# A state-space block and a maxout network on one core: another order of the opening, sixteen unread products, other tables for blocks zero and one

## The chip, the cores and the metric

The kernel runs on one core of a Trainium2 chip. The metric is the device time of one execution in microseconds; lower is better. A run gives one time; the numbers here are medians of a few runs, and one further execution is recorded by the hardware profiler.

Engines go by these names: PE is TensorE (matmul; PEld is its weight load), DVE is VectorE, ACT is ScalarE, POOL is GpSimd, SP is SyncE, which here issues nearly all transfers.

## What is computed

First a chunked state-space scan over x, with decays a and projections B and C (4 batches, 8 heads, 768 tokens, head width 32, state width 16). Its output, seen as 3072 tokens of 256 numbers, goes through a network whose hidden layer is the maximum of three products.

```python
for c in range(nc):
    la = log_a[:, :, sl]
    cum = np.cumsum(la, axis=-1)
    L = np.exp(cum[:, :, :, None] - cum[:, :, None, :]) * causal
    CB = np.einsum('bhin,bhjn->bhij', Cc, Bc)
    y_intra = np.einsum('bhij,bhjd->bhid', CB * L, xc)
    y_inter = np.einsum('bhin,bhnd->bhid', Cc, state) * np.exp(cum)[:, :, :, None]
    y[:, :, sl] = y_intra + y_inter
    Bx = np.einsum('bhjn,bhjd->bhjnd', Bc, xc) * decay_from_j[:, :, :, None, None]
    state = decay_full[:, :, None, None] * state + np.sum(Bx, axis=2)

h = np.maximum(np.maximum(x @ w1, x @ w2), x @ w3)
return (h @ w_out).astype(np.float32)
```

The weights w1, w2, w3 (256 by 768) and w_out (768 by 256) come as 64-bit floats and are decoded on the chip to 32 bits.

## The kernel before

The 768 tokens of a sequence are cut into six blocks of 128 (NC = 6), numbered zero to five. A block is one scan chunk of 128 tokens in all four batches and, for the network, 512 tokens.

**The order is written by hand.** The tile scheduler is off (`manual_schedule`); each engine does its instructions in the order in which the program emits them, and waits on semaphores where one needs another's result. That order is given by strings of short words. `begin` reads the words of the opening, `act` those of the lists FIRST (block zero's network: one entry behind each of 18 groups of products), SEAM and PRELUDE (between blocks zero and one), SECOND (block one: one entry behind each of 18 units), STEADY (blocks two to four) and LAST (block five).

**Opening.** The decays of block zero are needed as exp(cum_i - cum_j) in a tile L for each batch and head. For batches 0 and 1 TensorE makes the whole difference in PSUM: a mask (`spread_mask`, L398), the sums of token i (`spread_i`, L414) and those of token j (`spread_j`, L426); ScalarE takes the exponential (`first_exps`, L446). For batches 2 and 3 TensorE spreads only the i part (L414 again), GpSimd prepares the other with the mask (`below`, L433), VectorE adds them (`first_sums`, L441), and ScalarE takes the exponential. Meanwhile C and B of block zero come in halves of two batches (C0 is C of batches 0 and 1, and so on), are transposed on TensorE (L511) and copied out by ScalarE, C twice with a parity factor (L883), B once (L879). Scores (L584) are products of both; VectorE multiplies them into L (`scan_weight`, L592). For two of the four heads' pairs of batches 2 and 3 ScalarE copies the scores to SBUF (L890) and GpSimd multiplies (L892). Then come the outputs y of block zero (L627, copied at L634) and the state product A (L552).

The word `P` is a product that nobody reads: `pad` (L910) multiplies the identity with the mask into the PSUM bank of group 0, which group 0 overwrites later.

**Weights.** Twelve pieces of 512 KB are fetched by `fetch` (word W, L195). `decode` (word d) does two ScalarE passes (L220, L229), two VectorE passes (L221, L224) and an addition on GpSimd (L230); `sign` (word g) ends it on VectorE (L233). Group n of FIRST (four products, L683; groups 0 and 1 in halves, L675) needs piece n // 2. Its result is copied by ScalarE (L1166) or taken into a maximum by VectorE (L1170). From block one on each weight is used in three parts, made by the word w with the steps 0 (ScalarE, L267 and L269), 1 (L273 on VectorE or L277 on GpSimd) and 2 (L262); `WEIGHTS_DVE` lists the parts that go to VectorE.

**Running sums.** For the later blocks the decays' sums are scanned on VectorE (word r, L353), stored to DRAM (L895) and read back spread over the partitions as L tables (`decay_load`, L466, 1 MB each) and as E (`last_load`, L474, eight small transfers). GpSimd masks the tables (L478), ScalarE takes the exponentials in sets of four (word p, L485).

**Units.** In blocks one to five a unit is two products of the difference part (`unit_open`, L724), scaled in place by ScalarE (L710), and then four products of the other parts (L746). Units are opened ahead, in a ring of four PSUM banks. `LATE` names the units behind whose own products the next opening stands, instead of ahead of them; `COPIES` names those whose first result ScalarE copies (L756) rather than VectorE (L758). Down products (L783 for block zero, L788 later) lead to the output.

SP issues its transfers in program order, too; the prelude loop that fetches C, B, x and the first weight pieces stands ahead of everything else.

Of the kernel before, what the change touches and what calls it, by code (L numbers as in the profile page):

```python
# [20 lines left out]
def kernel(  # L21
# [22 lines left out]
    NB, NH, S, D = x.shape  # L44
    N = B.shape[-1]
    P = 128
    NC = S // P
# [26 lines left out]
    BACK = ((1.0 + TAU) / TAU) ** 2  # L74
    SMALL, LARGE = 2.0 ** -15, 122880.0 - 2.0 ** -7

    COPIES = {c: (0, 6, 7, 12,) if c == 1 else (1, 13,) for c in range(1, NC)}
    LATE = {c: (1, 2, 3, 5, 9, 13, 16, 17,) if c == 1 else (1, 3, 4, 6, 7, 9, 11, 14, 16, 17,) for c in range(1, NC)}
    WEIGHTS_DVE = ((0, 1), (0, 2), (1, 1), (1, 2), (3, 1), (4, 1), (4, 2), (6, 1), (7, 2), (8, 1), (9, 1), (9, 2), (10, 1), (10, 2), (11, 1),)

    const = ctx.enter_context(tc.tile_pool(name="const", bufs=1))
    raw = ctx.enter_context(tc.tile_pool(name="raw", bufs=1))
# [105 lines left out]
    def fetch():  # L188

        src, dt = weight_jobs.pop(0)  # L190
        rb = wraw.tile([P, 2, WCOL, 2], U32, tag="rb", name="rb")
        if dt == FP32:
            nc.sync.dma_start(out=rb[:, :, :, 0].bitcast(FP32), in_=src)
        else:
            nc.sync.dma_start(out=rb.rearrange("p k f w -> p k (f w)"), in_=src)  # L195
        fetched.append((rb, dt))
# [55 lines left out]
    def weight_parts(k):  # L252
# [6 lines left out]
        def last():  # L259
            d = wsum.tile([P, 2, WCOL], F32R, tag="w", name="wd")  # L260
            parts[k].append(d)
            (nc.vector if (k, 2) in WEIGHTS_DVE else nc.gpsimd).tensor_tensor(  # L262
                out=d.rearrange("p k f -> p (k f)"), in0=hi.bitcast(FP32), in1=lo.bitcast(FP32),
                op=ALU.subtract)

        def high():
            nc.scalar.activation(hi, w, AF.Copy, scale=HIGH * TAU)  # L267
            if (k, 1) not in WEIGHTS_DVE:
                nc.scalar.activation(lo, w, AF.Copy, scale=HIGH)  # L269

        def rest():
            if (k, 1) in WEIGHTS_DVE:
                nc.vector.scalar_tensor_tensor(  # L273
                    out=lo, in0=hi.bitcast(FP32), scalar=-1.0 / TAU, in1=w, op0=ALU.mult,
                    op1=ALU.add)
            else:
                nc.gpsimd.tensor_tensor(out=lo, in0=w, in1=lo.bitcast(FP32), op=ALU.subtract)  # L277
# [15 lines left out]
    def load_half(name, h):  # L293

        src = sources[name][0]
        if h == 0:
            load_tile(0, name)
        rows = slice(2 * h, 2 * h + 2)
        nc.sync.dma_start(  # L299
            out=blocks[0][name][:, 2 * h * NH:(2 * h + 2) * NH],  # L300
            in_=src[rows, :, 0:P, :].rearrange("b h s n -> s (b h) n"))

    for word in "C0 W B0 W C1 B1 x0 x1 W W".split():
        if word == "W":
            fetch()
        else:
            load_half(word[0], int(word[1]))
# [79 lines left out]
    def decays(c):  # L387
        Ls[c] = att.tile([P, NB, NH, P], FP32, tag="L", name="L")
        return Ls[c]
# [60 lines left out]
    L0, spread = decays(0), {}  # L450
# [278 lines left out]
    def unit():  # L729
# [3 lines left out]
        q, i = divmod(k, 3)  # L733
        late = 2 * k + g in LATE[c]

# [17 lines left out]
        if i == 0:  # L753
            m[g] = ffn.tile([P, BLK], FP32, tag="m", bufs=4, name="m")
            if 2 * k + g in COPIES[c]:
                nc.scalar.copy(out=m[g], in_=o)  # L756
# [230 lines left out]
        elif op in "GH":  # L987
            group_half(args[0], int(op == "H"))

    for word in ("k P v3 v2 C0 i2 q P i0 c0 d B0 u2 W j g b0 l e00 C1 P e10 e11 e01 s0 r x2 B1 x3 "  # L990
            "J i3 b1 c1 e21 s2 e20 x1 u3 e30 P x0 D W P P e31 y3 n y2 P X1 W o0 s3 z0 z1 W d "
            "A G0 o2 X0 W S L0 G1 H0 H1 N").split():
        begin(word)
    ncums = banks["ncums"]

# [69 lines left out]
    def plan(words, c, n):  # L1065
        for word in words.split():
            act(word, c, n)
# [4 lines left out]


    FIRST = [
        "g d d g f",
        "M11 W",
        "d M9 g",
        "F W M8 g d",
        "W",
        "d",  # L1080
        "M1 g m0,0 w0,0 t M0 b",
        "d C w1,0 M3",
        "w0,1 p0",
        "",
        "M4 d g p0",
        "g w1,1 d g p0 s0 x p0 w2,0",
        "w2,1 x w3,0 x g x",
        "",
        "E c m0,2",
        "w0,2 M2 d p0",  # L1090
        "s2 p0 B x x",
        "w1,2 M5 p0 p0 d g x w2,2 x g",
    ]
    SEAM = "y a a z z D w3,1 A x"
    PRELUDE = "b w3,2 B"
    SECOND = [
        "m0,0 E t w4,0 m0,2 C w5,0 w4,1 c w5,1 p0",
        "D",
        "",
        "w4,2 p0",  # L1100
        "w6,0",
        "w5,2 h p0 w7,0 s0 x w6,1 x r",
        "p0 w8,0 p0 D L w6,2 w9,0 w9,1",
        "",
        "h x w8,1 w7,1 p0 x D",
        "w10,0",
        "m1,0 p1 w7,2 r w8,2 s2 x p0",
        "h w9,2 m1,2 p0 x x",
        "w11,0 A p1",
        "w10,1 w10,2 x y x a z p1 a w11,1",  # L1110
        "w11,2 p1 z",
        "p1 h",
        "r",
        "l r",
    ]
    STEADY = [
        "t h E C b B c r",
# [38 lines left out]
    for n in range(NF * 3):  # L1156
        j, g = divmod(n, 2)
        q, i = divmod(j, 3)
        f = 2 * q + g
# [16 lines left out]
    downs += [(0, "0", b) for b in range(NB)]  # L1176
    plan(SEAM, 0, 1)
    plan(PRELUDE, 1, 2)
# [39 lines left out]
```

## Time and profile before

| | |
|---|---|
| runs | 275.38, 276.33, 277.6 us |
| median | 276.33 us |
| profiled execution, its own time | 276.44 us |
| its span, first to last instruction | 274.7 us |
| instructions in the span | 5403 |

The span is what the profile's times are counted in: they run from the first instruction. The rest of the profiled time lies around it. In the page a row of a group gives line, engine, operation, output and inputs, shapes and count, then busy time and mean length, then the engine's idle time ahead of those instructions and what ended it. The timeline merges like instructions in a row into one line, with the start and the length of the whole. A matmul in 32 bits is two records.

The costliest groups are the units' products: L746 with 96.6 us in 360 records, and L724 with 52.0 us in 180. The exponentials of the later blocks (L485) take 50.1 us of ScalarE in 160.

### The profile page before, as it was taken

The page shows a single profiled execution, that of the slowest core. Times are in us where ns is not written, and L with a number is a line of the kernel's source. Part 1 is how long each engine was busy: PE and PEld are TensorE (multiplying, and loading weights), DVE is VectorE, ACT ScalarE, POOL GpSimd, SP SyncE. Part 2 cuts the span into 40 slices and gives each one's busy share as a digit, 9 for nine tenths or more (in the row PEclk, how much of TensorE's full clock was granted, in tenths as well). Part 3 has the DMA queues.
Part 4 walks back from the last instruction along what each step waited for, and adds up shares of the span by engine and source line. Part 5 has one row for each costly group of instructions (what it writes and reads, how often), then busy time and mean ns, then how long its engine had stood idle before and what let it go on. Part 6 is the DMA issues. An engine that isn't in the chain of part 4 may idle for free.

```text
span 274.7 us, 5403 instructions
## 1 busy us (share of the span) xinstructions
PE 267.3 (97%) x2061; PEld 206.8 (75%) x2061; DVE 185.5 (68%) x299; ACT 180.8 (66%) x413; POOL 69.2 (25%) x69
## 2 busy tenths in 40 slices
PE   6999999998999999999999999999999999999995
PEld 3567454456878778879888879888889788899895
DVE  2554879999457799963488862588861787632882
ACT  4374949981989999736689736689744564534711
POOL 5215465655878502243000243000000000000000
PEclk9999999999999999999999999999999999999999
DMA  6899997959849685696250795200000100002002
GB/s 131 149 284 227 207 294 184 174 76 215 172 132 239 110 97 76 95 249 84 93 63 1 137 220 65 79 2 0 0 1 18 62 2 0 2 0 76 0 2 76
DMA packets 105097, 28.13 MB, mean 102 GB/s; under 512 B 75376, under 2 KB 102000, under 8 KB 105072
## 3 DMA queue, kind: packets, MB, share of 16 engines
q1 hardware_dynamic: 104768, 27.66, 50.3%
q8 instruction: 16, 0.26, 0.4%
q10 hardware_dynamic: 304, 0.13, 0.2%
q14 instruction: 9, 0.07, 0.1%
HBM read 24.54 MB, written 3.24 MB: 101 GB/s over the span
## 4 chain that ended last, share of the span: by engine, by line
PE 81%; SPq 8%; DVE 5%; DMA 2%; issue 2%; ACT 1%; ACTq 0%; DVEq 0%
PE up L746 31%; PE up L724 15%; PE o L788 13%; PE up L683 6%; SPq L195 5%; PE o L783 4%; PE s L584 4%; PE y L616 3%; SPq L299 2%; DMA raw_B<-in_B_dram 2%; PE o L815 2%; PE y L607 2%; DVE L L592 1%; PE A L552 1%; PE trB L511 1%
## 5 line engine op out<-in xcount | busy, mean ns | idle before, releaser
L746 PE MATMUL up<-six,wp 128*128 128x512 f32 x360 | 96.6, 396 | 0.0
L746 PEld LDWEIGHTS up<-six,wp 128*128 128x128 f32 x360 | 65.9, 188 | 15.0 <-issue 1.0
L760 DVE TENSOR_TENSOR m<-m,up 128x512 f32<-128x512 f32 x60 | 40.3, 684 | 42.6 <-PE up L746 42.2
L710 ACT ACTIVATE up<-up 128x512 f32<-128x512 f32 x90 | 50.6, 580 | 26.6 <-PE up L724 26.5
L724 PE MATMUL up<-six,wd 128*128 128x512 f32 x180 | 52.0, 396 | 0.0
L485 ACT ACTIVATE L<-L,ncums 128x128 f32<-128x128 f32 x160 | 50.1, 393 | 1.1 <-POOL L L478 1.1
L724 PEld LDWEIGHTS up<-six,wd 128*128 128x128 f32 x180 | 33.2, 188 | 8.7 <-issue 1.2
L592 DVE TENSOR_TENSOR L<-s,L 128x512 f32<-128x512 f32 x46 | 30.5, 685 | 9.3 <-PE s L584 8.0
L683 PE MATMUL up<-six,w 128*128 128x512 f32 x64 | 28.6, 598 | 0.7 <-DVE w L233 0.7
L478 POOL TENSOR_SCALAR_AFFINE_SELECT L<-L 128x1024 f32<-128x1024 f32 x20 | 22.9, 1166 | 10.0 <-DMA L<-cums 10.0
L788 PE MATMUL o<-wp,h 128*128 128x256 f32 x192 | 23.7, 283 | 0.0
L788 PEld LDWEIGHTS o<-wp,h 128*128 128x128 f32 x192 | 23.4, 192 | 0.1
L683 PEld LDWEIGHTS up<-six,w 128*128 128x128 f32 x64 | 11.8, 190 | 14.7 <-issue 11.8
L657 DVE SCALAR_TENSOR_TENSOR h<-h,h 128x512 fp32r<-128x512 f32 x30 | 21.7, 724 | 1.0
L230 POOL TENSOR_TENSOR h<-h,h 128x512 uint32<-128x512 uint32 x12 | 17.0, 1418 | 20.2 <-DVE h L224 19.3
L666 DVE TENSOR_TENSOR h<-m,h 128x512 fp32r<-128x512 f32 x30 | 21.2, 708 | 0.1
L663 ACT ACTIVATE h<-m 128x512 fp32r<-128x512 f32 x30 | 18.4, 629 | 3.6 <-DVE m L760 3.6
L801 ACT ACTIVATE ob<-o 128x512 f32<-128x512 f32 x10 | 6.0, 595 | 19.4 <-PE o L788 16.2
L758 DVE COPY m<-up 128x512 f32<-128x512 f32 x18 | 12.4, 687 | 7.3 <-PE up L746 7.3
L584 PE MATMUL s<-six,six 32*128 32x256 f32 x192 | 16.2, 401 | 0.0
L584 PEld LDWEIGHTS s<-six,six 32*128 32x128 f32 x192 | 10.3, 184 | 6.0 <-issue 2.4
L788 PEld LDWEIGHTS o<-wd,h 128*128 128x128 f32 x96 | 12.5, 190 | 0.7
(109 smaller groups left out, 313.7 us busy)
## 6 DMA issues: line engine op xcount, KB each, us to landing
L<-cums SPq DMA_DIRECT2D x10, 1024.0 KB, 9.4
rb<-in_moe_w_dram SPq DMA_DIRECT2D x9, 512.0 KB, 6.7
raw_x<-in_x_dram SPq DMA_DIRECT2D x5, 512.0 KB, 11.1
out_dram<-ob SPq DMA_DIRECT2D x10, 256.0 KB, 2.1
rb<-in_moe_w_out_dram SPq DMA_DIRECT2D x3, 512.0 KB, 8.1
raw_C<-in_C_dram SPq DMA_DIRECT2D x5, 256.0 KB, 6.1
raw_B<-in_B_dram SPq DMA_DIRECT2D x5, 256.0 KB, 4.2
E<-cums SPq DMA_DIRECT2D x40, 32.0 KB, 2.3
```

The costliest lines, as they stand in the source:

```text
L478: nc.gpsimd.affine_select(out=Ls[c][:, b], in_=Ls[c][:, b], pattern=[[0, NH], [1, P]], compare_op=ALU.is_ge, fill=MASKED, base=0, channel_ ...
L485: nc.scalar.activation(L[:, b, h], L[:, b, h], AF.Exp, bias=ncum[c][:, b * NH + h:b * NH + h + 1], scale=1.0)
L584: nc.tensor.matmul(out=s[:, i].rearrange("j g i -> j (g i)"), lhsT=st["BT"][rows, b], rhs=st["CT"][rows, :, b], start=(i == 0), stop=True, ...
L592: nc.vector.tensor_tensor(out=M, in0=s, in1=M, op=ALU.mult)
L657: nc.vector.scalar_tensor_tensor(out=out, in0=lo.bitcast(FP32), scalar=-1.0 / TAU, in1=hi.bitcast(FP32), op0=ALU.mult, op1=ALU.add)
L666: nc.vector.tensor_tensor(out=lo, in0=src, in1=hi.bitcast(FP32), op=ALU.subtract)
L683: nc.tensor.matmul(out=bank, lhsT=whole[3 * (f // 2) + i][:, k, f % 2 * P:(f % 2 + 1) * P], rhs=yT[0][:, k], start=(k == 0), stop=(k == KD ...
L710: nc.scalar.activation(bank, bank, AF.Copy, scale=-KAPPA)
L724: nc.tensor.matmul(out=o, lhsT=weight_part(k, 2, kk, cols), rhs=yT[c][2][:, kk], start=(kk == 0), stop=(kk == KD - 1), skip_group_check=True)
L746: nc.tensor.matmul(out=o, lhsT=weight_part(k, j, kk, cols), rhs=yT[c][j][:, kk], start=False, stop=(kk == KD - 1 and j == 1), skip_group_c ...
L760: nc.vector.tensor_tensor(out=m[g], in0=m[g], in1=o, op=ALU.max)
L788: nc.tensor.matmul(out=o[:, b % 2], lhsT=hs[f][p][:, tokens(b)], rhs=weight_part(NW + f // 2, p, f % 2, slice(0, DM)), start=(first and p ...
```

## The change

Seven places are edited; no function is.

1. The prelude loop of transfers: the first weight piece goes ahead of C0, the second behind x, and the other two of the four leave the loop for the opening.
2. The opening's words: the sums on TensorE (i0, j, i2) come directly behind the masks, ahead of the transposes of B and C; sixteen pads stand where seven were; the scan of the running sums (k, l, r) comes later; the loads of B and C of block one (X0, X1) and of the first L table (L0) move to FIRST; the second decode moves behind groups 0 and 1; weight pieces are fetched at other places.
3. FIRST: the decodes, signs, loads, weight parts, masks and scores stand behind other groups.
4. SEAM: the state product A ahead of the down product, and one order changed among the parts of y.
5. SECOND: the same words in another distribution.
6. `COPIES` and `LATE` for block one.
7. `WEIGHTS_DVE`: the parts (1,2), (4,2), (8,1), (9,1), (9,2) go to other engines, (5,2), (6,2), (7,1), (11,2) to VectorE.

```diff
-    COPIES = {c: (0, 6, 7, 12,) if c == 1 else (1, 13,) for c in range(1, NC)}
-    LATE = {c: (1, 2, 3, 5, 9, 13, 16, 17,) if c == 1 else (1, 3, 4, 6, 7, 9, 11, 14, 16, 17,) for c in range(1, NC)}
-    WEIGHTS_DVE = ((0, 1), (0, 2), (1, 1), (1, 2), (3, 1), (4, 1), (4, 2), (6, 1), (7, 2), (8, 1), (9, 1), (9, 2), (10, 1), (10, 2), (11, 1),)
+    COPIES = {c: (1, 7, 12,) if c == 1 else (1, 13,) for c in range(1, NC)}
+    LATE = {c: (3, 7, 9, 11, 12, 13, 14, 15, 16,) if c == 1 else (1, 3, 4, 6, 7, 9, 11, 14, 16, 17,) for c in range(1, NC)}
+    WEIGHTS_DVE = ((0, 1), (0, 2), (1, 1), (3, 1), (4, 1), (5, 2), (6, 1), (6, 2), (7, 1), (7, 2), (10, 1), (10, 2), (11, 1), (11, 2),)
...
-    for word in "C0 W B0 W C1 B1 x0 x1 W W".split():
+    for word in "W C0 B0 C1 B1 x0 x1 W".split():
...
-    for word in ("k P v3 v2 C0 i2 q P i0 c0 d B0 u2 W j g b0 l e00 C1 P e10 e11 e01 s0 r x2 B1 x3 "
-            "J i3 b1 c1 e21 s2 e20 x1 u3 e30 P x0 D W P P e31 y3 n y2 P X1 W o0 s3 z0 z1 W d "
-            "A G0 o2 X0 W S L0 G1 H0 H1 N").split():
+    for word in ("q i0 j v3 J i2 v2 P d e10 e11 B0 k u2 e00 g C0 c0 P b0 P e01 P l s0 B1 x0 P x1 P "
+            "C1 P c1 x3 P i3 P P P r e20 b1 D u3 s2 e21 P e31 P y2 s3 y3 e30 W x2 P z1 o0 P "
+            "z0 n A P o2 G0 G1 N H0 H1 S W d W W W").split():
...
     FIRST = [
-        "g d d g f",
-        "M11 W",
-        "d M9 g",
-        "F W M8 g d",
-        "W",
+        "g M6 M7 M10 W",
         "d",
-        "M1 g m0,0 w0,0 t M0 b",
-        "d C w1,0 M3",
-        "w0,1 p0",
-        "",
-        "M4 d g p0",
-        "g w1,1 d g p0 s0 x p0 w2,0",
-        "w2,1 x w3,0 x g x",
-        "",
-        "E c m0,2",
-        "w0,2 M2 d p0",
-        "s2 p0 B x x",
-        "w1,2 M5 p0 p0 d g x w2,2 x g",
+        "f W d g",
+        "d g",
+        "d F W M11 w0,0",
+        "d",
+        "M9",
+        "m0,0 g t g b w1,0 d g p0 m0,2",
+        "",
+        "w1,1 d C M8 W p0 w2,0 B E",
+        "w0,1 s0 W p0 x",
+        "g c w2,1",
+        "x w3,0 p0 p0 x g x w0,2 p0 w1,2 d",
+        "",
+        "",
+        "s2 d",
+        "M4 x x M0 w2,2",
+        "M3 p0 p0 M1 x g d M5 g x g M2",
     ]
-    SEAM = "y a a z z D w3,1 A x"
+    SEAM = "y a z A D a z w3,1 x"
     PRELUDE = "b w3,2 B"
     SECOND = [
-        "m0,0 E t w4,0 m0,2 C w5,0 w4,1 c w5,1 p0",
-        "D",
-        "",
-        "w4,2 p0",
-        "w6,0",
-        "w5,2 h p0 w7,0 s0 x w6,1 x r",
-        "p0 w8,0 p0 D L w6,2 w9,0 w9,1",
-        "",
-        "h x w8,1 w7,1 p0 x D",
-        "w10,0",
-        "m1,0 p1 w7,2 r w8,2 s2 x p0",
-        "h w9,2 m1,2 p0 x x",
-        "w11,0 A p1",
-        "w10,1 w10,2 x y x a z p1 a w11,1",
-        "w11,2 p1 z",
-        "p1 h",
-        "r",
-        "l r",
+        "w4,0 w4,1 w5,0 w6,0 E t c D w5,1 m0,0 C p0",
+        "",
+        "w6,1 L w4,2 w5,2 w7,0 s0 p0",
+        "w8,0",
+        "",
+        "p0 h",
+        "m1,0 w9,0 p0 m0,2",
+        "w9,1 x",
+        "x r x D p0 w6,2 w10,0 l p0 p0 w8,1 p1 x D w7,1 w7,2",
+        "",
+        "s2 m1,2 x w8,2 p1 x p0 x h w9,2",
+        "w11,0 x w10,1 p1",
+        "r w11,1 A x",
+        "w10,2 y a a z z p1",
+        "h",
+        "",
+        "w11,2 h r",
+        "r p1",
     ]
```

The words that the argument uses: P pad; q the factors from token j to the block's end (ScalarE, L361) and J their turn on TensorE; i0, i2, i3 the sums of batches 0 and 1, of 2, of 3; j the sums of token j; v below; u first sums; e an exponential (e10: batch 1, half 0); C, B, c, b transposes and copies; s scores; x, z score products on VectorE; y the same through GpSimd; o outputs; A state product; G, H halves of groups 0 and 1; M, L, X, E loads.

## The prediction

> **What bounds the kernel now.** I read the page first, then the chain of waits, then TensorE's timeline from the first product on, and last the timelines of ScalarE, VectorE and the SP queue for the same stretch. The page:
>
> ```profile
> span 274.7 us, 5403 instructions
> PE 267.3 (97%) x2061; PEld 206.8 (75%) x2061; DVE 185.5 (68%) x299; ACT 180.8 (66%) x413; POOL 69.2 (25%) x69
> PE 81%; SPq 8%; DVE 5%; DMA 2%; issue 2%; ACT 1%; ACTq 0%; DVEq 0%
> ```
>
> TensorE carries 81% of the chain; SPq carries only the first 31 us. The matmuls' ends are modelled, so the 97% proves little; the starts do. TensorE's timeline (start, length, instruction, count):
>
> ```profile
> 2.49 1.86 PE L398 MATMUL spread<-mask,ident 128*128 128x512 bf16 x4 [2.49 <-POOL mask L335]
> 5.70 2.08 PE L414 MATMUL spread<-a,pick 32*128 32x128 f32 x16
> 7.71 0.61 PE L910 MATMUL up<-mask,ident 128*128 128x512 bf16 x1
> 8.25 2.09 PE L414 MATMUL spread<-a,pick 32*128 32x128 f32 x32
> 10.27 0.69 PE L511 MATMUL tr<-ident,raw_B 128*128 128x128 f32 x2
> 10.89 2.09 PE L426 MATMUL spread<-npick,a 32*128 32x512 f32 x8
> 13.96 2.28 PE L584 MATMUL s<-six,six 32*128 32x256 f32 x16
> 16.17 0.44 PE L511 MATMUL tr<-ident,raw_B 128*128 128x128 f32 x2
> 19.07 0.82 PE L910 MATMUL up<-mask,ident 128*128 128x512 bf16 x3
> ...
> 27.62 3.68 PE L683 MATMUL up<-six,w 128*128 128x512 f32 x8
> 31.94 5.39 PE L683 MATMUL up<-six,w 128*128 128x512 f32 x12 [0.47 <-DVE w L233]
> ...
> 46.72 1.15 PE L584 MATMUL s<-six,six 32*128 32x256 f32 x16
> ...
> 63.60 0.41 PE L616 MATMUL y<-L,raw_x 128*32 128x128 f32 x4 [0.81 <-DVE L L592]
> ```
>
> Two things are to be seen. First, the sixteen rows of scores take 2.28 us at 13.96 and 1.15 us at 46.72; unread products start 0.54 us apart at 7.71 (next row 8.25) and 0.22 apart at 19.07 (three until 19.72). TensorE runs at half speed up to a point inside the row at 13.96; the single starts put it at about 15.3. The page's granted clock reads full all along and does not show this. Second, work follows on work: from 27.62 to 68.5 (first products of block one) I find, at single starts, gaps of 0.6 us (group 4 waits for a decoded weight at 31.9), 0.35 (47.5) and 1.3 (the y products at 62.5 to 64.2), and from 68.5 to the end only drains of some 0.1 us. So the end is the start of block one plus a fixed amount; a change must act before 68.5 us, or open gaps after it.
>
> [...] release came 12.8 us after the first product, with work queued throughout. [...] its longest stretch without a transpose or a half-filled array (L414 for one batch uses two of four row groups) is 2.5 us. [...] The landings agree: C0 5.04, W 7.45, B0 8.22, W 10.57, C1 11.59, B1 13.14, x 15.26 and 16.72, as issued.
>
> **The change, part by part.** Against the profiled execution: span 274.7, time 276.44, so 1.74 lie around it; 276.44 is within 0.1 of the median 276.33.
>
> *Opening, up to the first scores.* New order: masks, ncum, sums for batches 0 and 1 (L414, 2.02), L426 (2.02), from_j (0.25), sums for batch 2 (2.01), a pad (0.54), B0 and C0 transposes (0.62 each), three pads (1.6), scores. From 4.61: 4.61+2.02+2.02+0.25+2.01+0.54+1.24+1.6 = 14.3, at half clock throughout, against 13.96. No data wait enters: C0 and B0 land by 8.2 in either order, since the first weight piece only changes places with C0.
>
> *From the scores to the end of group 1* (27.62 before, where whole groups begin). Pads rise from 7 to 16; 12 stand behind the first scores against 4, so 8 x 0.22 = 1.7 us, and some 0.7 for drains (0.09 each at changes of shape). C1's transposes move behind the scores and from_j ahead: +0.1. With the clock released at 15.3 as before, group 1 ends at 27.6+0.3+1.7+0.7+0.1 = 30.4, **+2.8**.
>
> *The clock.* In the new order masks, sums and L426 stand back to back from 2.49 to 8.75, all four row groups filled, no transpose. If that is what the release wants, it comes at about 8.5. Then 6.8 us of half clock would save 3.4, but the scores can't start so early: they wait for ScalarE, which from L426's end (8.6) does three exps (L446, 0.52 each, until 10.2), then C0's two scaled copies (0.84) and B0's copy (0.37) after C0's transposes at 10.65: scores at 11.95, not 14.3, a gain of 2.3; and they and B1's transposes run warm, 0.9 more. Group 1 ends at about 27.2, **-0.4**. Behind them the order is TensorE's own: z and y products for o2 end at 20.7 (GpSimd 2 x 1.25 after s2), o2 is reached at 21.3.
>
> *Moves on queues.* On SP the first weight piece stands ahead of C0, the other early piece behind x, so C1, B1 and x land some 2 us earlier; nothing waited for them, 0. The store of the running sums (L895, 15.8 before) now waits for scans that VectorE does behind three score products, at 15.7 (early clock) to 18.7; queued behind it are five weight pieces, B and C of block one, and the L tables. At 1.6 us a piece (landings 18.92, 20.58, 22.20) the third piece lands at 21 and the seventh near 28; they are needed from group 1's end on, at 3.5 us a piece: 0, by 6 us or more. The L tables (3.6 us each) would land at about 33 and 42, and the second mask (L478) asks for its table at about 40 to 43; some 4 us of slack lie between it and the next decode on GpSimd: 0, at worst 1.
>
> *FIRST.* Decode 2 is issued after group 1's copy, no longer before it. Its path from group 1's end: ScalarE copy 0.6, L220 0.57, VectorE L221 and L224 0.9, GpSimd L230 1.3, then on VectorE behind group 2's maximum (0.68) and decode 3's pair (0.9) the sign step L233 (0.7): group 4 starts at +4.65 against +4.3 before (31.94-27.62), **+0.35**. The scores of block one (after group 10, before after 11) wait for CT, which ScalarE reaches behind copies, a decode and one set of four exps (1.2): 0.6 late, against 0.35 before, **+0.25**. At the seam the last exps, a decode and three sign steps stand before the last score product as they did: y waits about 1.2 (1.3 before), and state product A moves ahead of the down product, 0. With rounding in these chains, block one starts 41.7 after group 1 against 40.9, **+0.8**, between -1.0 (all gaps vanish but that at group 4) and +2.
>
> *Block one's tables.* LATE names units 3, 7, 9 and 11 to 16 in place of 1, 2, 3, 5 ...: the early units open two ahead before their own products, so a bank must come free one unit (0.93) earlier. ACT loses one copy (0.6) and gains one L269 (0.5); VectorE gains one copy (0.69) and loses one weight part (0.7). ScalarE is busy 41.0 of 43.5 us from 68.5 to 112, so order matters: after unit 8 it gets sixteen exps (5.1), a weight step, a hidden copy and an output copy, about 7.5 us, while TensorE has two down products (2 x 2.6), two units and scores, about 9. That holds. There is no gap to win here: floor 0, I take **+0.4**, up to +1.5. Blocks two to five run the same tables: 0.
>
> **Sum, likeliest case** (early clock): -0.4+0.8+0.4 = +0.8, 276.4+0.8 = **277.2**.
>
> **The rivals.**
> 1. *The clock is released no earlier.* For it: in the trace before, the sums and L426 at 8.25 to 12.9 filled the array and did not release it; the release fell in the first products with dense data on both sides, and those stand at 14.3 in the new order too. Against: no stretch before was as long as the new one. Then +2.8+0.8+0.4 = +4.0: 280.4. Each us of later release costs about 0.5; from a release at about 12.4 on, the whole is over 1% slower. [...]
> 2. *Early clock, and the hand-written order closes FIRST's gaps:* -0.4-1.0+0 = -1.4, 275.0. For it: before has 2.3 us of gaps there. Against: the longest hangs on ScalarE and VectorE work that is not less.
> 3. *A wait in block one:* a unit opened early waits for its bank or for a scaled copy behind exps, +1.5 there: 278.3 with the early clock. For it: ScalarE's 94%. Against: the down products cover the crowded places.
> 4. *The pads cost nothing, because they stand in waits:* then -0.4 becomes about -2, total 275.6. Against: in my order TensorE waits only once, 0.65 us before the scores.
>
> **Numbers.** Early clock with my sum 0.40, rival 1 with its half-way case 0.32, rivals 2 and 4 together 0.18, rival 3 0.10. The range reaches from 274.8 (rival 2, just under) to 280.6 (rival 1): the parts' bounds lie within it, and about 2 in 10 outside. One per cent is 2.8 us, about what a measurement of this kernel can tell: the three runs lie between 275.4 and 277.6. Over 1% slower (above 279.1): nearly all of the late release, 0.25, and a few of the others, 0.32 in all. Over 1% faster (below 273.6) needs an early clock, no gaps in FIRST and a release near 6.8 us together: 0.10. Within 1%: 0.58.
>
> **What would show it.** Release: score rows (L584) 72 ns each rather than 138 at the first scores, L414 for batch 2 in 1.0 us rather than 2.0. Opening: whole groups begin at about 27.2 (early) or 30.4 (late). FIRST: a gap before group 4's L683 released by L233; L724 of block one starts 41.7 after group 1. Block one: no idle row over 0.3 us from there to block two. I am wrong if groups begin before 26 with all sixteen pads in, if weights land late behind the store, or if block one shows gaps of over 1.5 us.

## The result and the profile after

The changed kernel takes 276.63 us (median of 12 runs, 275.43 to 277.47), the kernel before 276.32 us (median of 12, 275.38 to 277.6). The ratio is 1.0008 with a 95% interval of 0.9988 to 1.0028: no difference. The forecast was no change, 277.2 us between 274.8 and 280.6.

The profiled execution of the changed kernel spans 274.4 us against 274.7. From its page, the lines of span, of TensorE and of the chain by engine:

```profile
span 274.4 us, 5419 instructions
PE 264.4 (96%) x2070; PEld 205.8 (75%) x2070; DVE 187.3 (68%) x299; ACT 180.9 (66%) x413; POOL 72.4 (26%) x70
PE 85%; DMA 6%; DVE 4%; SPq 2%; ACT 1%; issue 1%; POOL 1%; ACTq 0%; POOLq 0%; DVEq 0%
```

The SP queue is hardly on the chain any more (8% before). TensorE's timeline of the opening (start, length, instruction, count, idle time ahead and who ended it):

```profile
4.46 2.17 PE L414 MATMUL spread<-a,pick 32*128 32x128 f32 x32
6.32 1.30 PE L426 MATMUL spread<-npick,a 32*128 32x512 f32 x8
...
7.49 1.13 PE L414 MATMUL spread<-a,pick 32*128 32x128 f32 x15
8.56 0.39 PE L910 MATMUL up<-mask,ident 128*128 128x512 bf16 x1
...
10.57 1.62 PE L584 MATMUL s<-six,six 32*128 32x256 f32 x16 [0.54 <-ACT six L879]
...
21.83 3.72 PE L675 MATMUL up<-six,w 128*128 128x256 f32 x16
26.32 3.67 PE L683 MATMUL up<-six,w 128*128 128x512 f32 x8 [0.77 <-DVE w L233]
30.58 1.96 PE L683 MATMUL up<-six,w 128*128 128x512 f32 x4 [0.59 <-DVE w L233]
```

L426 took 2.09 us before and takes 1.30: the clock is released inside it, ahead of the first pad at 8.56; the trace's list of clock changes, which begins with the release, has it at 6.78. The sums of batch 2 then take 1.1 us (2.1 before). The first scores start at 10.57 (13.96), and the halves of groups 0 and 1 end at 25.4 (27.6).

In the kernel before that list has the release at 13.90, ahead of the first scores, and not at 15.3 inside them, as the prediction read it. The pad in front of them is still at half speed (0.63 us against 0.39), but the score records last as long as in the changed kernel and as at 46.72. The pad of the kernel before, then the score records (count, shortest/median/longest in ns) before and after:

```profile
13.39 0.63 PE L910 MATMUL up<-mask,ident 128*128 128x512 bf16 x1
L584 PE MATMUL s<-six,six x16: 374/374/478, 14.0 to 15.9; 32*128 32x256 f32 x16
L584 PE MATMUL s<-six,six x16: 374/374/479, 10.6 to 11.8; 32*128 32x256 f32 x16
```

The row at 13.96 took 2.28 us because its products stood apart (by the profile their weight loads waited 1.0 us in all for ScalarE's exponentials, L446), not because of the clock.

In the changed kernel TensorE stands still twice behind the halves for a sign step, L233. Later in FIRST:

```profile
44.59 1.15 PE L584 MATMUL s<-six,six 32*128 32x256 f32 x16 [0.68 <-ACT six L526]
...
51.65 3.70 PE L683 MATMUL up<-six,w 128*128 128x512 f32 x8 [0.56 <-DVE w L233]
...
64.20 0.52 PE L616 MATMUL y<-L,raw_x 128*32 128x128 f32 x10 [1.05 <-DVE L L592]
...
68.26 1.61 PE L724 MATMUL up<-six,wd 128*128 128x512 f32 x6
```

The scores of block one wait for CT (C of block one, transposed and copied out, L526), a later group for another decoded piece, the y products for the last score product. Measured between starts, the gaps are 0.94, 0.75, 0.84, 0.73 and 1.21 us. Block one starts at 68.26, 0.3 us earlier than before:

```profile
68.55 1.63 PE L724 MATMUL up<-six,wd 128*128 128x512 f32 x6
```

In a table, times in us from the span's start:

| | before | after |
|---|---|---|
| first scores | 13.96 | 10.57 |
| halves of groups 0 and 1 end | 27.6 | 25.4 |
| from there to block one | 40.9 | 42.9 |
| block one starts | 68.55 | 68.26 |
| from there to the end | 206.2 | 206.1 |

So the opening won 2.2 us and FIRST gave 1.95 back. The experiments ask what released the clock, what the pads do, and whether FIRST's loss lies in its order.

A mean granted clock comes with every execution. It reads 1.0 in the kernel before in spite of the half speed at its start (pads 0.54 us apart at 7.71, 0.22 at 19.07): it tells only of drops after the first release. Where an experiment lets the clock drop, its runs spread widely; there all runs are given beside the ratio, which leaves the most disturbed out.

### The profile page after: what moved, and what is told of

Same layout as the page of the kernel before. It is cut to its first block, busy times and chain, and to the rows that moved or that the text cites. A ratio compares the mean times of both kernels' runs of the same rounds, so it can differ in the third digit from the quotient of the medians.

```text
span 274.4 us, 5419 instructions
## 1 busy us (share of the span) xinstructions
PE 264.4 (96%) x2070; PEld 205.8 (75%) x2070; DVE 187.3 (68%) x299; ACT 180.9 (66%) x413; POOL 72.4 (26%) x70
## 4 chain that ended last, share of the span: by engine, by line
PE 85%; DMA 6%; DVE 4%; SPq 2%; ACT 1%; issue 1%; POOL 1%; ACTq 0%; POOLq 0%; DVEq 0%
PE up L746 31%; PE up L724 15%; PE o L788 13%; PE s L584 5%; DMA L<-cums 4%; PE o L783 4%; PE y L616 3%; PE o L815 2%; PE up L683 2%; DMA raw_x<-in_x_dram 2%; PE y L607 2%; PE spread L414 1%; PE up L675 1%; PE up L910 1%; DVE L L592 1%; PE A L552 1%
## 5 line engine op out<-in xcount | busy, mean ns | idle before, releaser
L710 ACT ACTIVATE up<-up 128x512 f32<-128x512 f32 x90 | 50.5, 579 | 25.4 <-PE up L724 25.2
L683 PE MATMUL up<-six,w 128*128 128x512 f32 x64 | 29.1, 600 | 1.9 <-DVE w L233 1.9
L683 PEld LDWEIGHTS up<-six,w 128*128 128x128 f32 x64 | 11.6, 190 | 16.5 <-issue 11.5
L666 DVE TENSOR_TENSOR h<-m,h 128x512 fp32r<-128x512 f32 x30 | 20.5, 683 | 0.1
L758 DVE COPY m<-up 128x512 f32<-128x512 f32 x19 | 13.1, 687 | 9.6 <-PE up L746 9.6
L584 PE MATMUL s<-six,six 32*128 32x256 f32 x192 | 15.6, 401 | 1.2 <-ACT six L526 0.7
L542 POOL TENSOR_TENSOR raw_B<-raw_B,from_js 128x512 f32<-128x512 f32 x4 | 5.2, 1293 | 35.0 <-PE trB L511 35.0
```

Source lines behind the costliest of these rows:

```text
L584: nc.tensor.matmul(out=s[:, i].rearrange("j g i -> j (g i)"), lhsT=st["BT"][rows, b], rhs=st["CT"][rows, :, b], start=(i == 0), stop=True, ...
L666: nc.vector.tensor_tensor(out=lo, in0=src, in1=hi.bitcast(FP32), op=ALU.subtract)
L683: nc.tensor.matmul(out=bank, lhsT=whole[3 * (f // 2) + i][:, k, f % 2 * P:(f % 2 + 1) * P], rhs=yT[0][:, k], start=(k == 0), stop=(k == KD ...
L710: nc.scalar.activation(bank, bank, AF.Copy, scale=-KAPPA)
```

## The experiments

**One pad of sixteen.** All pads but the first leave the opening's string:

```diff
-    ("q i0 j v3 J i2 v2 P d e10 e11 B0 k u2 e00 g C0 c0 P b0 P e01 P l s0 B1 x0 P x1 P ...
+    ("q i0 j v3 J i2 v2 P d e10 e11 B0 k u2 e00 g C0 c0 b0 e01 l s0 B1 x0 x1 ...
```

> The changed kernel with one pad of its sixteen (the first) left in the opening. Theory A (the order of the sums releases the clock, the pads are filler): L414 for batch 2 still takes about 1.0 us, scores 72 ns a row or less, the clock stays up, the halves of groups 0 and 1 end 0.5 to 1.2 us earlier than the changed kernel's 25.4, and the time falls by 0.3 to 1.2 us to 275.4 to 276.3. Theory B (the pads hold the clock): some rows between the first scores and group 0 are at half speed again (scores 140 ns, L683 0.87 us apart), and the time rises by 1 to 3 us.

Six of seven runs lie at 274.23 to 274.92, with a granted clock of 0.993 to 1.0, one at 281.03 with 0.976; ratio 0.9936 (0.9912 to 0.996). The profile is that of the run at 281.03. Its stretches: length, TensorE's busy time and products, granted clock, share and rate of the transfers:

```profile
8.00:11.00 3.00, 1.93 (x26) 1.00 0.95 98
11.00:13.00 2.00, 1.88 (x15) 0.61 1.14 174
13.00:15.00 2.00, 2.00 (x8) 0.50 1.03 197
```

and its timeline there:

```profile
9.55 0.38 PE L511 MATMUL tr<-ident,raw_C 128*128 128x128 f32 x2
11.12 2.57 PE L584 MATMUL s<-six,six 32*128 32x256 f32 x16 [1.19 <-ACT six L879]
```

The clock was up by the first pad (the pad takes 0.39 us), then TensorE waits 1.19 us for copies of ScalarE, and from 11.4 to 25.1 it is at half speed again. So both theories hold in part: the release came early with one pad as with sixteen, as A has it, but in this run the clock fell behind a wait, as B has it. And where it falls for a short while only (five of the six runs have a mean of 0.993 or 0.994), leaving the pads out gains some 2 us.

**The sums first, alone, in the kernel before.**

```diff
-    ("k P v3 v2 C0 i2 q P i0 c0 d B0 u2 W j g b0 l e00 C1 P ...
+    ("k P v3 v2 i0 j C0 i2 q P c0 d B0 u2 W g b0 l e00 C1 P ...
```

> The kernel before with one edit: the sums of batches 0 and 1 and L426 directly behind the masks; seven pads, old transfers, old FIRST. Theory A: the clock is released between 6 and 8 us (15.3 before), groups 0 and 1 end 2 to 3.5 us before 27.6, decode 1 is early there, so most of it reaches block one: 273.5 to 275. Rival C (decodes and ScalarE chains in FIRST set block one's start whatever the opening does): opening earlier as above, but 275.5 to 276.5, with wider gaps ahead of L683. Theory B (pads matter for the release): release stays at 12 or later, 276 to 277.

The 14 runs reach from 274.53 to 282.13, with a median of 279.04; the ratio of 1.0005 (0.9966 to 1.0043) is that of the seven shortest. The timeline of a run with the clock at 1.0 (275.06):

```profile
7.01 1.61 PE L426 MATMUL spread<-npick,a 32*128 32x512 f32 x8
...
10.24 0.38 PE L511 MATMUL tr<-ident,raw_B 128*128 128x128 f32 x2
12.60 0.44 PE L511 MATMUL tr<-ident,raw_C 128*128 128x128 f32 x2 [1.98 <-DVE L L441]
```

The release is early here too (L426 in 1.61, batch 2 in 1.16), with seven pads and the old transfers, so neither sixteen pads nor the new transfers are needed for it. This run is what theory A expects, and block one starts 40.9 us after group 1 as before, against rival C. But C1's transposes now wait 1.98 us for a bank that VectorE still reads, and in most runs the clock falls; the profile, of a run in which it stays up, doesn't show where. The times follow the granted clock:

| granted clock | runs, us |
|---|---|
| 1.0 | 274.53, 274.91, 275.06 |
| 0.994, 0.988 | 276.78, 276.84 |
| 0.98 | 278.08, 278.14 |
| 0.975 | 279.95 to 280.26, six runs |
| 0.97 | 282.13 |

**The same with the wait filled**: eight more pads ahead of C1.

```diff
-    ... W g b0 l e00 C1 P e10 ...
+    ... W g b0 l e00 P P P P P P P P C1 P e10 ...
```

> The kernel sums_first_only with eight more pads in the one wait of 1.98 us that it had ahead of the transposes of C1 (8 x 0.216 = 1.7). If the wait is what drops the released clock (its runs had granted clocks of 0.97 to 1.0 and times of 274.5 to 282.1), then every run now has 0.998 or more and lies between 274.4 and 276. Rival (the drop comes from elsewhere, or the pads don't count as work): the spread stays over 3 us and the clock goes down to 0.98 or below in some runs.

```profile
9.79 1.89 PE L910 MATMUL up<-mask,ident 128*128 128x512 bf16 x8
11.94 0.44 PE L511 MATMUL tr<-ident,raw_C 128*128 128x128 f32 x2 [0.25 <-DVE L L441]
```

Eight runs at 274.36 to 275.81; ratio 0.9939 (0.9913 to 0.9966). Seven have a granted clock of 1.0. The eighth, which the profile shows, has 0.992: there the clock falls at 17.0, for 3.4 us (three pads at 16.88 take 1.35 us against 0.82 in the run above), without a wait, behind scores and sums that fill half the array. The expectation holds but for that one run: with the wait open the times reached from 274.5 to 282.1, with pads in it from 274.4 to 275.8.

**Half an array first.** In the changed kernel the sums of batch 2 go ahead.

```diff
-    ("q i0 j v3 J i2 v2 P ...
+    ("q i2 i0 j v3 J v2 P ...
```

> The changed kernel with the sums of batch 2, which fill two of four row groups, ahead of those of batches 0 and 1. Theory A1 (only a full array counts towards the release): [...] group 1 ends 1 to 1.7 us later, time up by 0.5 to 1.7. Theory A2 (any unbroken work counts): release at 6 to 7 as in the changed kernel, time within 0.4 of it.

Six runs at 279.96 to 283.27; ratio 1.0179 (1.0138 to 1.022).

```profile
8.00 2.01 PE L426 MATMUL spread<-npick,a 32*128 32x512 f32 x6
9.81 0.26 PE L369 MATMUL from_j_tp<-ident,fj 32*128 32x32 f32 x1
9.99 0.46 PE L910 MATMUL up<-mask,ident 128*128 128x512 bf16 x1
12.64 0.41 PE L511 MATMUL tr<-ident,raw_B 128*128 128x128 f32 x2 [2.19 <-issue]
```

L426's rows still start 0.85 us apart at 8.95; the clock list has the release at 10.17, not at 6.78. In the six other profiles with the changed order L426 ends between 7.4 and 8.3 and the clock is up by the first pad (0.39 us). In those six it is released at 6.41 to 8.82 behind the same instructions, so where it comes varies by itself; 10.17 lies outside that spread. TensorE's busy time in the 3.41 us ahead of the release at 6.78 in the changed kernel, and in the same stretch here (the granted clock of 1.00 hides the half speed, as said above):

```profile
3.37:6.78 3.41, 3.37 (x40) 1.00 1.03 218
3.34:6.75 3.41, 3.36 (x31) 1.00 1.01 221
```

Equally busy, but here with half-filled sums (L414 of batch 2, from 4.4 to some 6.3): no release until 10.17. That is what A1 expects; one trace of this order does not show that the half-filled sums are the cause. The time doesn't price it: the edit also makes B0's transposes wait 2.2 us, and the clock falls again, from 13.6 to 20.4 (scores from 14.46 take 2.57 us). A release also came with transposes among the products ahead of it: in the kernel before 0.9 of the 3.4 us ahead of 13.90 are transposes, and in the kernel with block one's tables alone (below), which has the same opening, 0.6 of those ahead of its release at 12.14. An opening without half-filled sums but with all the transposes was not tried.

**Decode 1 early.**

```diff
-    ... z1 o0 P z0 n A P o2 G0 G1 N H0 H1 S W d W W W
+    ... z1 o0 P z0 n d A P o2 G0 G1 N H0 H1 S W W W W
```

> The changed kernel with its second decode issued before the state product A instead of behind groups 0 and 1. If the wait for decode 1 ahead of group 2 (0.94 us in the changed kernel's profile) is a loss of its own, that gap goes and block one starts 0.5 to 0.9 earlier: 275.7 to 276.1. Rival: the waits behind it (group 4 for decode 2, scores for CT, y for the last score product) hang on ScalarE and VectorE chains and take it back: gap gone, the next ones wider, time within 0.3 of 276.6.

276.29 us, ratio 0.9999 (0.9979 to 1.002): the rival.

```profile
25.88 3.68 PE L683 MATMUL up<-six,w 128*128 128x512 f32 x8
31.07 1.95 PE L683 MATMUL up<-six,w 128*128 128x512 f32 x4 [1.52 <-DVE w L233]
```

The gap ahead of group 2 is gone, that ahead of group 4 has grown from 0.75 to 1.68, the sum of both. Group 4 starts 5.19 us behind group 1's end in either kernel: its decode stands on ScalarE behind group 1's copy, whatever stands ahead.

**Decodes 1 and 2 early.** Beside the edit above; decode 3 comes forward with decode 2, as in the kernel before:

```diff
-        "g M6 M7 M10 W",
-        "d",
-        "f W d g",
+        "g d d g M6 M7 M10 W",
+        "",
+        "f W",
```

> The changed kernel with its second decode ahead of A and its third and fourth directly behind the first entry's sign step, as in the kernel before (ScalarE then does them ahead of group 1's copy); all else is the changed kernel's. If the late decodes are what the new FIRST loses first, both gaps shrink to the old ones: none ahead of group 2, about 0.64 ahead of group 4 (0.94 and 0.75 in the changed kernel, 1.68 ahead of group 4 with decode 1 alone early); block one starts about 41.8 after group 1, and the time is 275.2 to 275.9. The waits for CT (0.84) and the last score product (1.2) stay, so it doesn't reach the 274.25 of the old FIRST. Rival: the later waits take it back: 42.5 or more, 276.2 or more.

```profile
26.14 3.68 PE L683 MATMUL up<-six,w 128*128 128x512 f32 x8
30.48 1.95 PE L683 MATMUL up<-six,w 128*128 128x512 f32 x4 [0.66 <-DVE w L233]
...
67.45 1.62 PE L724 MATMUL up<-six,wd 128*128 128x512 f32 x6
```

275.38 us, ratio 0.9959 (0.9944 to 0.9975). The gap ahead of group 4 is 0.82, the later one for a decoded piece (ahead of 51.65 in the changed kernel) is gone as well, and block one starts 41.3 after group 1. The waits for CT (0.82) and for y (1.21) stay, as expected.

**The changed opening with everything else of before.** The kernel before takes the new order of transfers and the opening's string; decode 1 stands ahead of A, and the two fetches and three loads that the old FIRST counts on follow at the end:

```diff
-    for word in "C0 W B0 W C1 B1 x0 x1 W W".split():
+    for word in "W C0 B0 C1 B1 x0 x1 W".split():
...
+    (the changed kernel's string as far as "z0 n", then)
+            "d A P o2 G0 G1 N H0 H1 S W W W W X1 X0 W W L0"
```

> The kernel before with the changed kernel's transfers and opening alone (sixteen pads, decode 1 ahead of A, the fetches and loads that the old FIRST counts on behind the opening); FIRST, SEAM, SECOND and the tables are those of before. Theory D (the opening gains 2 us and the new FIRST gives them back by waits on decodes 1 and 2, on CT and on the last score product): groups 0 and 1 end at 25.3 to 26, block one starts 40.5 to 41.5 later instead of 42.9, time 274.0 to 275.2. Rival E (FIRST's length follows ScalarE whatever its order): block one starts 42.5 or more after group 1, time 276 to 277.

274.25 us (273.84 to 275.09), ratio 0.9923 (0.9897 to 0.9949).

```profile
21.57 3.72 PE L675 MATMUL up<-six,w 128*128 128x256 f32 x16
25.13 3.67 PE L683 MATMUL up<-six,w 128*128 128x512 f32 x8
28.64 0.33 PE L369 MATMUL from_js_tp<-ident,fj 96*128 96x96 f32 x2
29.45 5.39 PE L683 MATMUL up<-six,w 128*128 128x512 f32 x12 [0.48 <-DVE w L233]
...
66.07 1.63 PE L724 MATMUL up<-six,wd 128*128 128x512 f32 x6
```

Group 2 follows at once, and block one starts 40.9 after group 1, to a tenth as in the kernel before: theory D. The opening's gain reaches the end whole where FIRST stays as it was.

**The tables of block one alone** (LATE, COPIES, WEIGHTS_DVE and SECOND of the change in the kernel before).

> The kernel before with LATE, COPIES, WEIGHTS_DVE and SECOND of the changed kernel, old opening and old FIRST. The traces of both show no gap over 0.25 us in block one, so: time within 0.4 of before, 275.9 to 276.7. Rival (the tables gain or lose what the rest of FIRST hides): more than 0.6 either way.

276.97 us (22 runs), ratio 1.0022 (1.0003 to 1.0042): 0.6 us slower, the interval only just away from none, and just outside what was expected. The profiled run, at 279.66, is one with a dropped clock (19.0 to 22.4) and no measure of the whole, but behind the drop it shows two waits that are longer than before:

```profile
65.58 0.41 PE L616 MATMUL y<-L,raw_x 128*32 128x128 f32 x4 [1.47 <-DVE L L592]
...
97.76 1.13 PE L584 MATMUL s<-six,six 32*128 32x256 f32 x10 [0.79 <-ACT ob L801]
```

The first (0.81 before) stands at FIRST's end; WEIGHTS_DVE also moves a part that the old FIRST makes, (1,2), from VectorE to GpSimd. The second stands in block one, where the kernel before has none. How the 0.6 of the medians is shared between them one run can't tell. In the changed kernel's own profile block one to the end is as long as before.

**The pads up to the scores.** In the changed kernel the first four pads stay, the twelve behind the first scores go.

> The changed kernel with the first four pads, all ahead of the first scores, and none of the twelve behind them. Theory F (the pads hold the released clock only across the wait ahead of the first scores): no run above 278 and the mean granted clock at 0.994 or more in all, time 274.0 to 275.0, that is the twelve later pads cost about 2 us. Rival (the waits behind the scores drop the clock as well): several runs at 0.975 to 0.988 and 276 to 281, as one run with one pad had.

Eight runs at 273.9 to 275.57, clock 1.0 but once (0.992); median 274.78, ratio 0.9934 (0.991 to 0.9958): theory F, nearly to the letter. With the first pad alone the clock was 1.0 in one run of seven, with the three pads directly ahead of the first scores in seven of eight. TensorE now waits in the open:

```profile
11.57 1.63 PE L584 MATMUL s<-six,six 32*128 32x256 f32 x16 [0.54 <-ACT six L879]
...
15.49 2.29 PE L584 MATMUL s<-six,six 32*128 32x256 f32 x16 [0.62 <-ACT six L879]
...
20.22 1.08 PE L627 MATMUL y<-L,raw_x 128*32 128x128 f32 x32 [0.53 <-DVE L L592]
21.23 3.72 PE L675 MATMUL up<-six,w 128*128 128x256 f32 x16
```

From the first scores to the end of group 1's halves it takes 13.2 us against 14.8. Twelve pads of 0.216 are 2.6; about 1 of that stood in waits that now lie open, and 1.6 was on the path.

**The new opening with four pads, the old rest.**

> The kernel opening_only with the first four pads alone. If theories D and F both hold the gains add: groups 0 and 1 end at 23.3 to 24.3, block one starts about 41 later, time 272.3 to 273.8. If the weights' landings or the decodes then bound FIRST (piece 2 landed at 20.2 in the changed kernel and its decode takes some 4 us), the gaps ahead of L683 widen and the time stays at 274 to 275.

```profile
24.10 3.67 PE L683 MATMUL up<-six,w 128*128 128x512 f32 x8
...
65.08 1.63 PE L724 MATMUL up<-six,wd 128*128 128x512 f32 x6
```

273.37 us (six runs, 272.98 to 273.56), ratio 0.9885 (0.9862 to 0.9909): the gains add, and this version is faster than both kernels. Groups 0 and 1 end at 24.1, block one starts 41.0 later. Three of the six runs have a mean clock of 0.994, and are no slower.

## Why the prediction was right, and which terms were not

- *The bound* was right: the time is block one's start plus 206 us (206.0 to 206.3 in ten of the twelve profiles, 206.75 with decode 1 early, 207.4 with block one's tables alone), and what an edit brings is read there.
- *The clock.* The likeliest case held: with the full-array stretch put first the release came earlier. Rival 1 fell. The size was off: 6.78 in the profile, not 8.5, which was the author's estimate and shown by no trace, and between 6.41 and 8.82 in all profiles with that order. The old release was misread, too: 13.90, 11.4 us after the first product, not 15.3 and 12.8. So the sums at 8.25 to 12.9, which rival 1 took for a full-array stretch without effect, stand directly ahead of it, and the scores with dense data on both sides, from 13.96 on, come behind it; and the sign of 72 ns a score row could not come, since these rows took 101 ns (1.62 us for 16) at full clock. Transposes, which it took as a likely hindrance, make up 0.6 to 0.9 us of the 3.4 ahead of the release in the two profiles of the old opening; in the one trace with half-filled sums first it came at 10.17. That the released clock fell again (at 11.4 in the profile with one pad), and that with three more pads in the changed kernel it stayed at 1.0 in seven runs of eight, was not in the prediction at all; it took the pads for filler. The sentence on rival 4, that pads cost something since TensorE waits only once, holds: 1.6 us on the path. That rival's -2 for the opening is near the measured -2.2 all the same, but for another reason, the next point.
- *The opening, -0.4*, measured -2.2. The term was mis-sized by 1.8. Of that 0.8 is the earlier release: in the four profiles with sixteen pads in this order the clock came at 6.41, 6.78, 7.88 and 8.33 and groups 0 and 1 ended at 25.13, 25.38, 25.88 and 26.14, half a us per us, which makes 26.2 at 8.5. The other 1.0 was a fault of the working: its own order reached o2 at 21.3, to which o2 (1.0) and the halves (3.7) add up to 26.0, while the sum, which counted drains for each pad, said 27.2. Two routes to one number should have been laid side by side. The 0.9 for scores and transposes that run at full clock was no gain, as they did so before; without it the forecast would have been further off.
- *FIRST, +0.8*, measured +1.95. The step on decode 2 was right in kind: L683 of group 4 is released by L233, 5.2 after group 1 rather than 4.65. It left out decode 1, which the change moves behind groups 0 and 1 as well, and so the 0.94 ahead of group 2; with an opening that ends earlier, nothing hides it. Of the later waits, CT was put at 0.6 (0.84), y at 1.2 (1.21), and the wait for a piece ahead of 51.65 (0.73) was not seen.
- *Block one's tables, +0.4*, measured 0 in the changed kernel (206.1 against 206.2), and no idle row over 0.25 us there. Alone in the old kernel they go with some 0.6 more.
- *Queues.* Nothing came late behind the store: the third piece landed at 20.2 and the seventh at 26.0 (21 and 28 estimated), the L tables at 34.9 and 43.2 (33 and 42). All of it at no cost, as put down.
- *The sum.* -0.4+0.8+0.4 = +0.8 was forecast; the profile has -2.2+1.95-0.05 = -0.3, and the medians +0.3. That the total was close was luck: two errors of 1.8 and 1.2 had opposite signs. The verdict, no change, was right for a reason that the prediction named (the opening gains, FIRST gives back), with both parts too small.

## What to carry to other kernels

If the first products of a kernel run at half speed, look at what stands between them: here the products that fill the whole array, put first, came with a release at 6.4 to 8.8 us against 12.1 and 13.9. Then look for the first waits behind it, here of 1.2 to 2.2 us, and try unread products in them: with one pad the granted clock was 1.0 in one run of seven, with four in seven of eight (with four and the old FIRST in one of six, the others 0.994 to 0.999). Further ones are paid for where TensorE bounds the path (twelve cost 1.6 us here). And when an opening gets shorter, the work of other engines that was hidden behind it has to move with it; here decodes placed later took most of the gain away (block one starts 42.9 us after group 1 with them late, 41.3 with them early, 40.9 with the old FIRST).

## What the runs showed of the hardware

- With full-array sums directly behind the masks the clock was released 3.9 to 6.3 us after the first product (nine profiles; 4.2 in the changed kernel's). With transposes and half-filled sums between them it took 11.4 us in the kernel before and 9.7 with block one's tables alone (the same opening), with half-filled sums first 7.7. In one pair of traces a stretch of 3.41 us of full-array products (3.37 us busy) was followed by a release, an equally busy one with half-filled sums (3.36) was not.
- A wait of 1.19 us was followed by a fall of the clock in the profile with one pad (at 11.4), one of 2.19 in that with half an array first (at 13.6); one of 1.98 in that with the sums first was not. What decides this is not shown. In two profiles (the wait filled, at 17.0; block one's tables alone, at 19.0) the clock fell without a wait, behind half-filled sums and scores.
- In the four profiles with a fall the clock stayed down for 3.41 us (the wait filled, block one's tables alone), 6.83 (half an array first) and 13.65 (one pad). A mean clock of 0.994 over 273 us is 3.3 us at half speed. What a fall costs differs: 276.78 with a mean clock of 0.994 against 274.5 to 275.1 with 1.0 where the sums alone stand first, nothing to be seen with one pad (274.23 to 274.59 against 274.92). The runs of the kernel with the sums alone first spread by 7.6 us, from 274.53 (clock 1.0) to 282.13 (0.97).
- The granted clock of the page does not show half speed ahead of the first release (1.0 in the kernel before, released at 13.90); the distance between starts does (pads 0.54 us apart ahead of it, 0.22 behind it), and the trace's list of clock changes begins with the release.
